# RWKV readout of the state: one f32 product, or three float32r products of split parts

## The chip, the cores and the metric

One core of a Trainium2 chip runs the whole program. The metric is the device time of one execution in microseconds; of the kernel before there are three runs, and one further execution under the hardware profiler. The engines by their names in the profile: PE is TensorE's matmuls, PEld its weight loads, DVE is VectorE, ACT is ScalarE, POOL is GpSimd, SP issues the DMAs.

## What is computed

A linear attention with a decaying state over 768 tokens (4 batches, 8 heads of 48), and behind it two gated feed-forward layers over all 3072 tokens. All inputs are float32.

```python
for t in range(S):
    kt, vt, rt = (k[:, :, t], v[:, :, t], r[:, :, t])
    cur = np.einsum('bhd,bhe->bhde', u[None] * kt, vt)
    y[:, :, t] = np.einsum('bhd,bhde->bhe', rt, state + cur)
    state = w[None, :, :, None] * state + np.einsum('bhd,bhe->bhde', kt, vt)
...
a = x @ w_a
b = x @ w_b
x = a * b @ w_out
...
h = (x @ w1) * (x @ w2) @ w3
return h @ w_out2
```

## The kernel before

The 768 tokens are cut into six steps of 128. A unit `u` (0 to 23) is one batch in one step: step `u // 4`, batch `u % 4`. In a unit each head's work is a masked 128x128 score matrix (`scores`, L380), its product with v (L420), the product of r with the state from the steps before (L416), and the new state (`s_mm`, L481; `s_decay` on ACT, L488; `s_upd` on DVE, L498). Two heads lie side by side in one 112-row tile (rows 0 to 47 and 64 to 111), so the state of a batch is four 112x112 blocks, and L416 is four products of a 112x112 block by 112x128 columns of r. These attention products have plain f32 operands. The products of the feed-forward layers (L631, L684 to L686, L798, L821 to L823) take float32r operands: each float32 tensor is kept as a high part (the value rounded to float32r, written by an ACT cast) and a low part (the rest, written by a DVE subtraction), and a product is the sum of three: high by high, high by low, low by high.

The order of the work is written out by hand. `merge` (L537) goes through the slots of the feed-forward layer's tiles and deals the attention's slots of the next step out between them, so that PE has feed-forward products to do while DVE, ACT and POOL get a unit's operands ready. The eight slots of a unit are in `unit_slots` (L510): scores; masking (`a_evac`, L391) on DVE; writing the diagonal (`a_diag`, L397) on DVE; then, two slots later, `y_mm` and `s_mm` on PE; then the loads of the unit two further on, and `y_evac` on ACT and DVE. Steps 2 to 5 (units 8 to 23) are dealt out over runs with different numbers of slots: in step 2 a unit takes about 10 us, later about 20 us. In these steps POOL prepares the next unit: r by powers of the decay (L352), k likewise (L356), then `k_nat` (L373) and the two products for the diagonal (L361, L363).

`Stream` (L56) brings the feed-forward weights in: a DMA into a staging buffer (`stg_t`, four buffers of 4 KB a partition in the pool `stg`), then an ACT cast and a DVE subtraction (L133, L154). Between its last weight of the first layer, at about 170 us, and its first of the second layer, after 500 us, it does nothing, and the staging buffers are empty. r and k of a unit come in one buffer `rk` (two of them, in turn); the load for unit u+2 (L214, on SP's queue) waits until the last reader of unit u's buffer is done. The tile `at` in PSUM has two buffers and carries scores, y and the state's increment in turn.

Of the kernel before, what the change touches and what calls it, by code (L numbers as in the profile page):

```python
# [8 lines left out]
F32R = mybir.dt.float32r  # L9
# [4 lines left out]
ALU = mybir.AluOpType  # L14
# [4 lines left out]
B, H, S, D = 4, 8, 768, 48  # L19
NP = H // 2  # L20
C = 128
# [7 lines left out]
NF2 = F2 // 128  # L29
NB = NC  # L30
TB = B * C
HALF = C // 2

W_LO, W_HI = 0.72, 1.25
# [142 lines left out]
def rwkv_moe_kernel(ctx, tc, rkT, nat, wu, wab, wout, w12, w3T, wo2, r_in, k_in, v_in, w_in, u_in, out):  # L177
    nc = tc.nc
    mm = nc.tensor.matmul

    dram = ctx.enter_context(tc.tile_pool(name="dram", bufs=1, space=DRAM))
    y_d = dram.tile([B, S, DM], F32, name="y_d")
    m_d = [dram.tile([128, KD, TB], F32, name=f"m_d{q}") for q in range(NB)]

    def flat(ap):
        return ap.rearrange("p a b -> p (a b)")

    with tc.manual_schedule():
# [4 lines left out]
        stg = tc.alloc_tile_pool(name="stg", bufs=Stream.AHEAD, side="right")  # L193
# [16 lines left out]
        def load_rk(u):  # L210
            if u < NU:
                rk_t[u] = (wabp.tile([112, 2, NP * C], F32, tag=("w1h", "w1l", "w2h", "w2l")[u], name="rk")
                           if u < B else att.tile([112, 2, NP * C], F32, name="rk"))
                nc.sync.dma_start(out=rk_t[u], in_=rkT[u])  # L214
# [3 lines left out]
        def load_nat(u):  # L218
            if u < B:
                nc.sync.dma_start(out=v_0[:, u, :], in_=nat[u, :, 2, :])  # L220
            elif u < NU:
                nat_t[u] = att.tile([128, 3, DM], F32, name="natt")
                nc.sync.dma_start(out=nat_t[u], in_=nat[u])
# [101 lines left out]
        nc.vector.tensor_scalar(out=wc, in0=wt, scalar1=W_LO, scalar2=W_HI, op0=ALU.max, op1=ALU.min)  # L325
        zer = const.tile([112, HALF], F32, name="zer")
        nc.vector.memset(zer, 0.0)
        tmp = wabp.tile([112, 1024], F32, tag="w3l", name="tmp")
        pos = tmp[:, 512:512 + NP * (HALF + 1)].rearrange("p (n c) -> p n c", n=NP)
        tkw = tmp[:, 0:512].rearrange("p (n c) -> p n c", n=NP)  # L330
        nc.vector.memset(pos[:, :, 0:1], 1.0)
        for p in range(NP):
            nc.vector.tensor_tensor_scan(
                out=pos[:, p, 1:], data0=wc[:, p:p + 1].to_broadcast([112, HALF]), data1=zer,
                initial=1.0, op0=ALU.mult, op1=ALU.add)
        tr = att.tile([112, NP, C], F32, name="tr", bufs=1)
        nc.vector.tensor_copy(out=tr[:, :, HALF:], in_=pos[:, :, 0:HALF])
        nc.vector.reciprocal(out=tr[:, :, 0:HALF], in_=pos[:, :, 1:][:, :, ::-1])
        tk = att.tile([112, NP, C], F32, name="tk", bufs=1)
        nc.vector.tensor_copy(out=tk, in_=tr[:, :, ::-1])  # L340
        wC = const.tile([112, NP, 1], F32, name="wC")
        nc.vector.tensor_tensor(out=wC, in0=pos[:, :, HALF:], in1=pos[:, :, HALF:], op=ALU.mult)
        s_t = [att.tile([112, NP, 112], F32, name=f"s{b}", bufs=1) for b in range(B)]

        rf_t, d_t, a_t, kn_t, at_ps, xt = {}, {}, {}, {}, {}, {}

        kf_t, pr_t, y3_t = {}, {}, {}

        def prep_r(u, eng):
            r = rk_t[u][:, 0, :]  # L350
# [17 lines left out]
        def k_nat(u):  # L368
            if u < NU - B:
                k = k_0[:, u, :] if u < B else nat_t[u][:, 1, :]  # L370
                kn_t[u] = k if u < B else att.tile([128, DM], F32, name="kn", bufs=1)
                eng = nc.vector if u < 2 * B - 1 else nc.gpsimd
                eng.tensor_tensor(out=kn_t[u], in0=k, in1=tnat.rearrange("p a x d -> p (a x d)"), op=ALU.mult)  # L373

        def scores_f(ps, r, k):

            for p in range(NP):
                s = slice(p * C, (p + 1) * C)
                for x, (r0, r1) in enumerate(XR):
                    mm(ps[x][:, p, :], lhsT=k[r0:r1, s], rhs=r[r0:r1, s], start=True, stop=True)  # L380

        def scores(u):
            for x in range(2):
                at_ps[u, x] = ps_at.tile([128, NP, C], F32, name="at")
            scores_f([at_ps[u, x] for x in range(2)], flat(rf_t[u]), kf_t.pop(u))

        def a_evac(u, hf):
            if hf == 0:
                a_t[u] = (wop.tile([128, H, C], F32, tag=("woh1", "wol1")[u % 2], name="a_0")
                          if u < B else att.tile([128, H, C], F32, name="a_sc", bufs=1))  # L390
            nc.vector.tensor_tensor(  # L391
                out=a_t[u][:, 4 * hf:4 * hf + 4, :], in0=at_ps.pop((u, hf)),
                in1=mask.rearrange("p (o n) -> p o n", o=1).to_broadcast([128, 4, C]), op=ALU.mult)

        def a_diag(u, hf):
            d = d_t[u].rearrange("p (q x) -> p x q", x=2)[:, hf, :]
            nc.vector.copy_predicated(  # L397
                out=a_t[u][:, 4 * hf:4 * hf + 4, :],
                mask=ident.bitcast(I32).rearrange("p (o n) -> p o n", o=1).to_broadcast([128, 4, C]),
                data=d.rearrange("p (h o) -> p h o", o=1).to_broadcast([128, 4, C]))  # L400

        def diag_0(u):

            for x in range(2):
# [2 lines left out]
                    mask=ident.bitcast(I32).rearrange("p (o n) -> p o n", o=1).to_broadcast([128, 4, C]),  # L407
                    data=at_ps.pop(("d", u, x)))

        def y_mm(u):  # L410
            c, b = divmod(u, B)
            ps = at_ps["y", u] = ps_at.tile([112, NP, C], F32, name="at")
            v, a = nat_t[u][:, 2, :], a_t.pop(u)

            for p in range(NP):
                mm(ps[:, p, :], lhsT=s_t[b][:, p, :], rhs=rf_t[u][:, p, :], start=(p == 0), stop=False,  # L416
                   skip_group_check=True)
            for h in range(H):
                r0, r1 = XR[h % 2]
                mm(ps[r0:r1, h // 2, :], lhsT=v[:, h * D:(h + 1) * D], rhs=a[:, h % 2 * 4 + h // 2, :],  # L420
                   start=False, stop=True, skip_group_check=True)
            rf_t.pop(u)
# [16 lines left out]
        def y_0_evac(u):  # L439
            if u == 0:  # L440
                xt[0] = xtp.tile([128, 2, KD, TB], F32R, tag=X_TAG[0], name="xt")
            ps = at_ps.pop(("y", u))
# [4 lines left out]
        def y_evac(u):  # L447
            c, b = divmod(u, B)
            if b == 0:
                xt[c] = xtp.tile([128, 2, KD, TB], F32R, tag=X_TAG[c], name="xt")  # L450
                y3_t[c] = att.tile([112, 2, TB], F32R, name="y3", bufs=1)
            xh, xl = xt[c][:, 0], xt[c][:, 1]
# [8 lines left out]
        def y_shuffle(c):  # L461

            for r0 in (0, 64):
                for k in range(KD):
                    nc.sync.dma_start(out=xt[c][r0 + 48:r0 + 64, :, k, :].bitcast(F32),
                                      in_=y3_t[c][r0 + 16 * k:r0 + 16 * k + 16].bitcast(F32))

        def s_mm(u):
            c, b = divmod(u, B)
            v = v_of(u)  # L470
            nat_t.pop(u, None)
            if c == NC - 1:
                return
            ps = (ps_at.tile([112, NP, D], F32, name="at") if c else
                  ps_m.tile([112, NP, D], F32, tag=("m2", "m0")[u % 2], name="s_ps"))
            at_ps["s", u] = ps
            kn = kn_t.pop(u)
            for p in range(NP):
                for x, (r0, r1) in enumerate(XR):
                    hs = slice((2 * p + x) * D, (2 * p + x + 1) * D)  # L480
                    mm(ps[r0:r1, p, :], lhsT=kn[:, hs], rhs=v[:, hs],  # L481
                       start=True, stop=True)
# [27 lines left out]
        def unit_slots(u):  # L510
            n = u + 1
            nxt = n < NU
            pool = nc.vector if n < 2 * B else nc.gpsimd

            def after(f, *a):
                if nxt:
                    f(n, *a)

            return [
                lambda: (scores(u), after(prep_r, pool)),  # L520
                lambda: (a_evac(u, 0), a_evac(u, 1), after(prep_k, pool)),
                lambda: (a_diag(u, 0), a_diag(u, 1), k_nat(u)),
                lambda: after(prep_d, 0),

                lambda: (y_mm(u), s_mm(u)),
                lambda: (load_rk(u + 2), load_nat(u + 2), y_evac(u), (u + 1) % B == 0 and y_shuffle(u // B), s_decay(u),
                         after(prep_d, 1)),
                lambda: s_upd(u),
                lambda: after(prep_d, 2),
            ]  # L530
# [103 lines left out]
        def ab_slots(x, wget, keep):  # L634
# [3 lines left out]
            def run_a():  # L638
                w, ca, _ = wget()
                t["a"] = ps_ab.tile([128, TB], F32, name="ab")  # L640
                ab_mm(t["a"], w, ca, x())

            def run_b():
                w, _, cb = wget()
                t["b"] = ps_ab.tile([128, TB], F32, name="ab")
                ab_mm(t["b"], w, cb, x())
# [483 lines left out]
```

## Time and profile before

| | us |
|---|---|
| median of three runs | 918.27 |
| the three runs | 917.95, 918.27, 923.23 |
| the profiled execution, its own time | 921.02 |
| its span, first to last instruction | 919.2 |
| PE busy in the span | 889.4 (97%) |
| DVE, ACT, POOL busy | 449.9, 325.2, 106.9 |

The span is what the profile covers; 1.8 us of the profiled execution lie around it. Busy PE time is the union of its records, whose ends are modelled, so distances between starts tell more than durations. One f32 product appears as two PE records (and two weight loads), one float32r product as one of each.

### The profile page before, as it was taken

The numbers are of one execution on the slowest core, as the hardware profiler recorded it, in microseconds if no ns is written. First come the engines' busy times: TensorE is split into PE (matmuls) and PEld (weight loads), VectorE is DVE, ScalarE is ACT, GpSimd is POOL, SyncE is SP. The second block draws the span as 40 slices with busy tenths as digits, with TensorE's granted clock in tenths as the row PEclk, the third lists the DMA queues.
The fourth block names the chain that finished last, engine by engine and source line by source line (L and its number), as shares of the span: only waits on it lengthen the run. The fifth ranks groups of instructions, "written<-read, shape, count | busy, mean of one in ns | idle before, by whom it ended". The sixth has DMA issues, their size and how long they took to land.

```text
span 919.2 us, 12479 instructions
## 1 busy us (share of the span) xinstructions
PE 889.4 (97%) x4962; PEld 754.2 (82%) x4962; DVE 449.9 (49%) x762; ACT 325.2 (35%) x737; POOL 106.9 (12%) x104
## 2 busy tenths in 40 slices
PE   8877999999999999999999999999999999999997
PEld 7665788888888888888888888899988888888886
DVE  8998876356343333433332889566222222223212
ACT  3554565332222232222112778564322222222211
POOL 2204200036033213211100000000000000000000
PEclk9798899999999999999999999999999999999999
DMA  8654531024131221122103555352010101000001
GB/s 263 193 160 138 135 118 63 1 79 154 30 101 46 63 68 59 47 63 81 47 1 109 165 156 172 109 176 71 12 58 11 47 24 47 24 35 1 35 0 38
DMA packets 26065, 73.56 MB, mean 80 GB/s; under 512 B 3152, under 2 KB 7376, under 8 KB 26000
## 3 DMA queue, kind: packets, MB, share of 16 engines
q1 hardware_dynamic: 26000, 72.70, 26.1%
q8 instruction: 41, 0.67, 0.3%
q14 instruction: 24, 0.20, 0.1%
HBM read 61.28 MB, written 9.44 MB: 77 GB/s over the span
## 4 chain that ended last, share of the span: by engine, by line
PE 90%; DVE 6%; issue 1%; DMA 1%; ACT 1%; SPq 0%
PE ab L631 52%; PE m L684 5%; PE m L686 5%; PE m L685 5%; PE at L798 4%; PE o L822 3%; PE o L823 3%; PE o L821 3%; PE at L420 2%; PE at L380 2%; PE at L416 2%; DVE cvt L117 1%; DMA rk<-in_rkT_dram 1%; PE at L823 1%; PE at L821 1%
## 5 line engine op out<-in xcount | busy, mean ns | idle before, releaser
L656 DVE TENSOR_TENSOR ab<-g,ab 128x512 f32<-128x512 f32 x120 | 83.5, 696 | 305.2 <-PE ab L631 272.8
L631 PE MATMUL ab<-xt,w12h 128*128 128x512 f32 x576 | 177.4, 389 | 0.0
L650 ACT COPY g<-ab 128x512 f32<-128x512 f32 x120 | 70.4, 587 | 264.0 <-PE ab L631 263.9
L657 ACT CAST gh<-ab 128x512 fp32r<-128x512 f32 x120 | 70.5, 588 | 253.5 <-DVE ab L656 253.5
L631 PEld LDWEIGHTS ab<-xt,w12h 128*128 128x128 f32 x576 | 107.5, 188 | 18.8
L662 DVE TENSOR_TENSOR gl<-ab,gh 128x512 fp32r<-128x512 f32 x120 | 83.0, 691 | 61.5 <-ACT gh L657 60.8
L631 PE MATMUL ab<-xt,w12l 128*128 128x512 f32 x288 | 112.0, 389 | 0.0
L684 PE MATMUL m<-gh,woh 128*128 128x512 f32 x216 | 85.5, 396 | 0.4 <-ACT woh L133 0.4
L686 PE MATMUL m<-gh,wol 128*128 128x512 f32 x216 | 84.3, 390 | 0.8 <-DVE wol L154 0.8
L685 PE MATMUL m<-gl,woh 128*128 128x512 f32 x216 | 84.3, 390 | 0.0
L631 PEld LDWEIGHTS ab<-xt,w12l 128*128 128x128 f32 x288 | 54.1, 188 | 11.3
L352 POOL TENSOR_TENSOR rk<-rk,tr 112x512 f32<-112x512 f32 x16 | 20.7, 1294 | 281.5 <-DMA rk<-in_rkT_dram 140.3
L631 PE MATMUL ab<-xt,wab0h 128*128 128x512 f32 x144 | 48.0, 415 | 3.1 <-DVE xt L445 2.5
L684 PEld LDWEIGHTS m<-gh,woh 128*128 128x128 f32 x216 | 40.5, 188 | 10.2 <-ACT woh L133 0.8
L686 PEld LDWEIGHTS m<-gh,wol 128*128 128x128 f32 x216 | 40.5, 188 | 9.8 <-DVE wol L154 1.2
L685 PEld LDWEIGHTS m<-gl,woh 128*128 128x128 f32 x216 | 40.6, 188 | 8.3
L631 PE MATMUL ab<-xt,wab1h 128*128 128x512 f32 x144 | 46.9, 408 | 0.0
L631 PE MATMUL ab<-xt,wab4h 128*128 128x512 f32 x144 | 45.5, 397 | 0.0
L631 PE MATMUL ab<-xt,wab3h 128*128 128x512 f32 x144 | 45.5, 397 | 0.0
L631 PE MATMUL ab<-xt,wab2h 128*128 128x512 f32 x144 | 45.4, 397 | 0.0
L631 PE MATMUL ab<-xt,wab5h 128*128 128x512 f32 x144 | 45.0, 394 | 0.0
L117 DVE SCALAR_TENSOR_TENSOR cvt<-stg_t,cvt 128x512 int32<-128x512 int32 x61 | 44.6, 731 | 0.3
(275 smaller groups left out, 1582.2 us busy)
## 6 DMA issues: line engine op xcount, KB each, us to landing
natt<-in_nat_dram SPq DMA_DIRECT2D x20, 576.0 KB, 5.0
rk<-in_rkT_dram SPq DMA_DIRECT2D x24, 448.0 KB, 3.8
stg_t<-in_wab_dram SPq DMA_DIRECT2D x18, 512.0 KB, 4.0
stg_t<-in_w3T_dram SPq DMA_DIRECT2D x16, 512.0 KB, 3.9
stg_t<-in_w_dram SPq DMA_DIRECT2D x12, 512.0 KB, 3.7
stg_t<-in_wout_dram SPq DMA_DIRECT2D x9, 512.0 KB, 3.6
m_d<-m_sb SPq DMA_DIRECT2D x18, 256.0 KB, 3.2
stg_t<-m_d SPq DMA_DIRECT2D x18, 256.0 KB, 2.7
```

The source lines that it names most:

```text
L117: nc.vector.scalar_tensor_tensor(out=f, in0=w[:, :, 1], scalar=-0x40000000, in1=f, op0=ALU.bitwise_and, op1=ALU.bitwise_or)
L631: mm(ps, lhsT=w[i][:, k, cs], rhs=x[:, j, k, :], start=(n == 0), stop=(n == 3 * KD - 1))
L650: nc.scalar.copy(out=t["g"], in_=t["a"])
L656: nc.vector.tensor_tensor(out=t["b"], in0=g, in1=t["b"], op=ALU.mult)
L657: nc.scalar.copy(out=gh, in_=t["b"])
L662: nc.vector.tensor_tensor(out=gl, in0=t["b"], in1=gh, op=ALU.subtract)
L684: mm(m_ps[q][k], lhsT=wh[:, j, cs], rhs=gh, start=first, stop=False)
L685: mm(m_ps[q][k], lhsT=wh[:, j, cs], rhs=gl, start=False, stop=False)
L686: mm(m_ps[q][k], lhsT=wl[:, j, cs], rhs=gh, start=False, stop=last)
L798: mm(f_ps[i], lhsT=w3_t[i][a][:, g, :], rhs=wo2_t[g // 4][b][:, g % 4, :], start=(n == 0), stop=(n == 3 * NF2 - 1))
L821: mm(o_ps[q][b], lhsT=ph[:, cs], rhs=wh, start=(f == 0), stop=False)
L823: mm(o_ps[q][b], lhsT=pl[:, cs], rhs=wh, start=False, stop=(f == NF2 - 1))
```

## The change

From unit 8 on (`RS = 2 * B`) r by the state is computed as three float32r products for each of the four blocks. `split_rs` makes the parts in two tiles of the staging pool: in the slot of the scores ACT casts the state and r to their high parts; in the slot of the masking DVE subtracts for the state's low part; in the slot of the diagonal DVE subtracts for r's low part. Units 4 to 7 keep the f32 product.

```diff
--- before.py
+++ after.py
@@ -29,6 +29,7 @@
 NF2 = F2 // 128
 NB = NC
 TB = B * C
+RS = 2 * B
 HALF = C // 2
 
 W_LO, W_HI = 0.72, 1.25
@@ -344,7 +345,7 @@
 
         rf_t, d_t, a_t, kn_t, at_ps, xt = {}, {}, {}, {}, {}, {}
 
-        kf_t, pr_t, y3_t = {}, {}, {}
+        kf_t, pr_t, y3_t, rs_t = {}, {}, {}, {}
 
         def prep_r(u, eng):
             r = rk_t[u][:, 0, :]
@@ -407,14 +408,34 @@
                     mask=ident.bitcast(I32).rearrange("p (o n) -> p o n", o=1).to_broadcast([128, 4, C]),
                     data=at_ps.pop(("d", u, x)))
 
+        def split_rs(u, part):
+
+            s = s_t[u % B]
+            if part == 0:
+                t = stg.tile([112, 2, NP, 112], F32R, tag="stg_t", name="s_hl")
+                r = stg.tile([112, 2, NP, C], F32R, tag="stg_t", name="r_hl")
+                rs_t[u] = t[:, 0], t[:, 1], r[:, 0], r[:, 1]
+                nc.scalar.copy(out=rs_t[u][0], in_=s)
+                nc.scalar.copy(out=rs_t[u][2], in_=rf_t[u])
+            elif part == 1:
+                nc.vector.tensor_tensor(out=rs_t[u][1], in0=s, in1=rs_t[u][0], op=ALU.subtract)
+            else:
+                nc.vector.tensor_tensor(out=rs_t[u][3], in0=rf_t[u], in1=rs_t[u][2], op=ALU.subtract)
+
         def y_mm(u):
             c, b = divmod(u, B)
             ps = at_ps["y", u] = ps_at.tile([112, NP, C], F32, name="at")
             v, a = nat_t[u][:, 2, :], a_t.pop(u)
 
+            if u < RS:
+                terms = [(s_t[b], rf_t[u])]
+            else:
+                sh, sl, rh, rl = rs_t.pop(u)
+                terms = [(sh, rh), (sh, rl), (sl, rh)]
             for p in range(NP):
-                mm(ps[:, p, :], lhsT=s_t[b][:, p, :], rhs=rf_t[u][:, p, :], start=(p == 0), stop=False,
-                   skip_group_check=True)
+                for i, (s, r) in enumerate(terms):
+                    mm(ps[:, p, :], lhsT=s[:, p, :], rhs=r[:, p, :], start=(p == 0 and i == 0), stop=False,
+                       skip_group_check=True)
             for h in range(H):
                 r0, r1 = XR[h % 2]
                 mm(ps[r0:r1, h // 2, :], lhsT=v[:, h * D:(h + 1) * D], rhs=a[:, h % 2 * 4 + h // 2, :],
@@ -516,10 +537,14 @@
                 if nxt:
                     f(n, *a)
 
+            def rs(part):
+                if u >= RS:
+                    split_rs(u, part)
+
             return [
-                lambda: (scores(u), after(prep_r, pool)),
-                lambda: (a_evac(u, 0), a_evac(u, 1), after(prep_k, pool)),
-                lambda: (a_diag(u, 0), a_diag(u, 1), k_nat(u)),
+                lambda: (scores(u), after(prep_r, pool), rs(0)),
+                lambda: (a_evac(u, 0), a_evac(u, 1), after(prep_k, pool), rs(1)),
+                lambda: (a_diag(u, 0), a_diag(u, 1), k_nat(u), rs(2)),
                 lambda: after(prep_d, 0),
 
                 lambda: (y_mm(u), s_mm(u)),
```

In PE's order around unit 8, the first that is changed, this stands before: the feed-forward product m (`m` from `gh`, `gl` and the weights `woh`, `wol`), r by the state, scores by v, the state's increment, and the next feed-forward product.

```order
L686 MATMUL m_1246<-gh,wol_1451 128x512
L416 MATMUL at<-rk,s_168 112x128 x4
L420 MATMUL at<-a_sc,natt 48x128 x8
L481 MATMUL at<-natt,kn 48x48 x8
L631 MATMUL ab<-xt,wab3h 128x512 x2
```

And now, at the same place:

```order
L711 MATMUL m_1246<-gh,wol_1451 128x512
L437 MATMUL at<-r_hl,s_hl 112x128 x12
L441 MATMUL at<-a_sc,natt 48x128 x8
L502 MATMUL at<-natt,kn 48x48 x8
L656 MATMUL ab<-xt,wab3h 128x512 x2
```

Four f32 products have become twelve float32r products; nothing else on PE has moved. In DVE's order of the same unit (`a_sc` are the masked scores, `ab` and `gl` belong to a feed-forward tile, `y` and `xt` are the unit's output) this stands before:

```order
L391 TENSOR_TENSOR a_sc<-at,mask 128x512 x2
L397 COPY_PREDICATED a_sc<-ident,dg 128x512 x2
L656 TENSOR_TENSOR ab<-g,ab 128x512
L662 TENSOR_TENSOR gl<-ab,gh 128x512
L458 TENSOR_TENSOR y_1733<-at,y_1733 112x128
```

And now:

```order
L392 TENSOR_TENSOR a_sc<-at,mask 128x512 x2
L421 TENSOR_TENSOR s_hl<-s_168,s_hl 112x448
L398 COPY_PREDICATED a_sc<-ident,dg 128x512 x2
L423 TENSOR_TENSOR r_hl<-rk,r_hl 112x512
L681 TENSOR_TENSOR ab<-g,ab 128x512
L687 TENSOR_TENSOR gl<-ab,gh 128x512
L479 TENSOR_TENSOR y_1747<-at,y_1747 112x128
```

One subtraction stands between masking and diagonal, the other behind the diagonal, both ahead of the feed-forward tile's work.

## Rows read from the trace of the kernel before

**Rows 1.** Windows: busy us of each engine, granted clock (PEclk), DMA share, GB/s.

```profile
100.00:120.00 20.00, 18.88 (x82) 14.85 (x81) 19.14 (x27) 13.18 (x33) 6.51 (x5) 1.00 0.60 158
200.00:220.00 20.00, 20.00 (x167) 16.51 (x166) 12.48 (x21) 7.22 (x19) 12.75 (x12) 1.00 0.47 146
```

**Rows 2.** Timeline of PE, units 8 to 11: start us, us, line, tiles, records.

```profile
191.34 1.04 PE L416 MATMUL at<-rk,s 112*112 112x128 f32 x8
...
201.38 1.04 PE L416 MATMUL at<-rk,s 112*112 112x128 f32 x8
...
211.21 0.39 PE L686 MATMUL m<-gh,wol 128*128 128x512 f32 x1
211.44 1.04 PE L416 MATMUL at<-rk,s 112*112 112x128 f32 x8
212.40 1.08 PE L420 MATMUL at<-a_sc,natt 128*48 128x128 f32 x16
...
221.38 1.04 PE L416 MATMUL at<-rk,s 112*112 112x128 f32 x8
222.35 1.34 PE L420 MATMUL at<-a_sc,natt 128*48 128x128 f32 x15
```

**Rows 3.** Line L416: count, and ns of one record (min/median/max).

```profile
L416 PE MATMUL at<-rk,s x160: 270/272/421, 46.2 to 486.9; 112*112 112x128 f32 x160
```

**Rows 4.** Timeline of PE, f32 records with 128 weight and 112 moving columns.

```profile
26.07 0.94 PE L607 MATMUL tn_ps<-ident,tmp 112*128 112x112 f32 x7
```

**Rows 5.** Timeline of PE, float32r records with 384 moving columns.

```profile
584.23 0.85 PE L798 MATMUL at<-wo20l,w30h 128*128 128x384 f32 x4
584.92 0.85 PE L798 MATMUL at<-wo21l,w30h 128*128 128x384 f32 x4
```

**Rows 6.** PEld by line and form: weight loads, busy us, mean ns.

```profile
L631 PEld LDWEIGHTS ab<-xt,w12h 128*128 128x128 f32 x576 | 107.5, 188 | 18.8
```

**Rows 7.** Timeline of DVE, the diagonal's two writes and what follows, units 8 to 11.

```profile
188.41 1.38 DVE L397 COPY_PREDICATED a_sc<-ident,dg 128x512 f32<-128x512 int32 x2
189.67 0.70 DVE L656 TENSOR_TENSOR ab<-g,ab 128x512 f32<-128x512 f32 x1
...
198.36 2.29 DVE L397 COPY_PREDICATED a_sc<-ident,dg 128x512 f32<-128x512 int32 x2
200.55 0.69 DVE L656 TENSOR_TENSOR ab<-g,ab 128x512 f32<-128x512 f32 x1
...
208.40 3.32 DVE L397 COPY_PREDICATED a_sc<-ident,dg 128x512 f32<-128x512 int32 x2
211.61 0.70 DVE L656 TENSOR_TENSOR ab<-g,ab 128x512 f32<-128x512 f32 x1
...
220.51 2.16 DVE L397 COPY_PREDICATED a_sc<-ident,dg 128x512 f32<-128x512 int32 x2
222.56 0.70 DVE L656 TENSOR_TENSOR ab<-g,ab 128x512 f32<-128x512 f32 x1
```

**Rows 8.** Timeline of POOL, units 9 and 10.

```profile
198.55 1.50 POOL L373 TENSOR_TENSOR kn<-natt,tnat 128x384 f32<-128x384 f32 x1
200.01 1.49 POOL L361 TENSOR_TENSOR pr<-natt,u_bc 128x384 f32<-128x384 f32 x1
...
210.10 1.01 POOL L361 TENSOR_TENSOR pr<-natt,u_bc 128x384 f32<-128x384 f32 x1
```

**Rows 9.** Lines L154 and L133: a subtraction and a cast of 512 columns.

```profile
L154 DVE TENSOR_TENSOR w12l<-cvt,w12h x12: 680/689/693, 511.9 to 541.8; 128x512 fp32r<-128x512 f32 x12
...
L133 ACT CAST w12h<-cvt x12: 606/612/642, 509.9 to 541.2; 128x512 fp32r<-128x512 f32 x12
```

**Rows 10.** Waits of SP's queue: who waited for whom, us, times, longest.

```profile
SPq L214 <- PE at L416: 251.1, 14, 46.6
```

**Rows 11.** Timeline of DVE, a unit of step 3.

```profile
244.19 1.37 DVE L397 COPY_PREDICATED a_sc<-ident,dg 128x512 f32<-128x512 int32 x2
```

**Rows 12.** Timeline of PE, the same unit.

```profile
248.15 1.04 PE L416 MATMUL at<-rk,s 112*112 112x128 f32 x8
```

## The prediction

> **What bounds the kernel now.** I read the windows first: in steps 2 to 5 the matmul engine is never idle, and in the stretch in which the first changed units lie it is busy for all 20 of 20.00 us at a granted clock of 1.00, which is the 2.4 GHz level, while DVE is busy for 12.5 us and POOL for 12.8 us [rows 1]. So a microsecond added to PE's row in these steps is a microsecond of the kernel, and work on ACT or DVE costs nothing as long as it is done before PE wants it. Next, PE's timeline for one block of r by the state: eight records, started 110 ns apart (the run is 1.04 us long and its last record 0.27 us: 0.77 us over seven distances), and from the first of them to the first record of scores by v it is 0.96 us (211.44 to 212.40) [rows 2, 3]. Last, the timelines of DVE and POOL just ahead of these blocks, for what the new operands have to fit into [rows 7, 8].
>
> **What is removed and added on PE.** In 16 units (8 to 23) eight f32 records go and twelve float32r records come, each with its weight load of 112 columns. The trace has no float32r product with 128 moving columns; I bound one from four sides.
>
> By the moving side: float32r records with 384 columns start 172 ns apart (0.69 us for four), with 512 columns 230 ns apart (211.21 to 211.44) [rows 2, 5]. A straight line through the two gives 172 - 256 x 58/128 = 56 ns for 128 columns.
>
> By the weights: seven f32 records with 128 weight columns and only 112 moving columns start 112 ns apart (0.94 us less one record of 0.27 us, over six) [rows 4]. By their stream alone they would need 110 x 112/128 = 96 ns, so there the weight load sets the pace, not the stream. If that goes with the weight columns, 112 of them take 112 x 112/128 = 98 ns. The type doesn't change a load: a float32r load of 128 columns is the 188 ns record of the feed-forward products [rows 6].
>
> Like the f32 record that it replaces: 110 ns. If a load can't run beside the record before it: 188 ns, the length of a load's record. Like a float32r record of 512 columns, should short ones be no quicker: 230 ns.
>
> I take 98 ns, because the row that it comes from is the only one that shows a record whose weights outlast its stream, which these are by far. Then the block is eleven distances of 98 ns = 1.08 us and the last record to the next product. That end is 0.96 - 7 x 0.110 = 0.19 us now, and shorter by 110 - 56 = 54 ns with one pass in place of two: 0.14 us. Together 1.22 us instead of 0.96 us, +0.26 us, and for 16 units **+4.2 us**. By the other bounds: 56 ns gives 0.76 us and -3.3 us; 110 ns gives 1.35 us and +6.2 us; 188 ns 2.26 us and +20.8 us (with the whole end of 0.19 us); 230 ns 2.72 us and +28 us.
>
> The page "TensorE: Matmul & The Clock Gate" of the Trainium skill, under LDWEIGHTS, says that a load takes its columns divided by 1.2 in ns, whatever the rows. That is 93 ns for 112 columns and speaks against this change as the rows do; by it the block would be about 55 ns shorter than by mine and the term some 0.9 us smaller.
>
> **What is added on ACT and DVE.** Two casts and two subtractions a unit, of 448 and 512 columns; 512 columns cost ACT 612 ns and DVE 689 ns [rows 9]. ACT casts early, in the slot of the scores, with r ready a unit before; I cost it at nothing, and were this cover gone a late cast would delay the first subtraction by up to 1.2 us. DVE is another matter: the last subtraction must be done before the second product of the block, and it stands behind the masking and the diagonal, in order. What waits for it is PE itself, with everything behind it.
>
> From the start of the diagonal's first write to the block's start there are in units 8 to 11: 191.34 - 188.41 = 2.93 us, 201.38 - 198.36 = 3.02, 211.44 - 208.40 = 3.04, and 221.38 - 220.51 = 0.87 [rows 2, 7]. The two writes alone take 1.26 us (188.41 to 189.67) [rows 7], and the two subtractions add about 1.3 us, so 2.56 us are wanted: by themselves they fit in three of the four units and are 1.69 us late in unit 11.
>
> But POOL works at the same time in units 9 to 11. There the two writes took 2.19, 3.21 and 2.05 us instead of 1.26 (198.36 to 200.55, 208.40 to 211.61, 220.51 to 222.56), and POOL's instructions 1.49 us instead of 1.01 [rows 7, 8]: an instruction of one waits for one of the other. The subtractions read both operands from SBUF too, and I expect the same of them. Unit 9: 0.93 us of such waiting for two instructions, twice that for four: 2.56 + 1.86 - 3.02 = 1.4 us late. Unit 10: here the two writes already waited 1.95 us, and little is left of POOL's work behind them, so that alone: 2.56 + 1.95 - 3.04 = 1.5 us. Unit 11: 2.56 + 0.79 - 0.87 = 2.5 us, of which PE waits about 0.3 us already (its records of scores by v there take 1.34 us instead of 1.08) [rows 2]: 2.2 us. **Waits: 5.1 us.** Between 1.4 us (POOL never in the way: unit 11 alone, 1.69 less 0.3) and 8.4 us (in each of the units 9 to 11 about 1 us more than I took). In steps 3 to 5 there is room: 248.15 - 244.19 = 3.96 us in a unit where the two writes took 1.37 us without POOL beside them [rows 11, 12], so nothing is charged.
>
> The page "SBUF — State Buffer" of the Trainium skill, under "SBUF: two separate sides", says that a DVE instruction with two SBUF inputs and a GpSimd instruction shut each other out for their whole length. The stretched rows agree with that, and by it each of the four instructions could stand behind one whole POOL instruction, which is how the 8.4 us come about.
>
> **DMA and staging.** The load of r and k for unit u+2 waits for the last reader of unit u's buffer; that was the block on PE [rows 10] and is now the subtraction ahead of it, so the load goes a little earlier or as late as PE's new wait; POOL's work moves with it, which is why unit 9's overlap can't be read off exactly. The staging buffers hold no weights in these steps, and the first weights of the second layer come after the last block, so the stream loses nothing.
>
> **Sum.** +4.2 us and +5.1 us = +9.3 us. On the profiled execution's 921.02 us (span 919.2 and 1.8 around it) this is 930.3 us; its time lies 2.75 us over the median of 918.27 us, and on that the forecast is 927.6 us, +1.0%. About 1% (9.2 us) is what a measurement of this kernel can tell from no change.
>
> **The rivals.** *Three passes instead of four* (chance 0.12): the records are bound by the stream, 56 ns apart, the term is -3.3 us, and with waits from 1.4 to 5.1 us the end is between 916.4 and 920.1 us: no slower. For it: one float32r record has half the stream of one f32 record. Against it: the records whose weights outlast their stream [rows 4]. It decides from about 75 ns a record on downward, where a block is no longer than now. The page "FP8 and Floating Point Precision", section TensorE Precision Notes, of the Trainium skill counts a true f32 product as four passes; three for four is what this rival amounts to.
>
> *Waits hidden* (0.18): PE pays 4.2 us, but POOL's work, started earlier, is through before DVE's, and only unit 11 waits: 918.27 + 4.2 + 1.4 = 923.9 us. For it: the earlier load. Against: the load of the operands of L361 comes after the unit's last product, and that is not earlier.
>
> *Short float32r records are dear* (0.13): 188 to 230 ns each, +20.8 to +28 us, with the waits 944 to 951 us. For it: no row shows one shorter than 172 ns. Against: f32 records with loads as long start 110 to 112 ns apart, so loads do overlap.
>
> **How the numbers follow.** The forecast has the remaining 0.57; its own range is 923 to 933 us (waits 1.4 to 8.4, records 98 to 110 ns), about six tenths of it over 1%. Slower by over 1%: 0.34 + 0.13 = 0.47. Faster by over 1%: none of the cases gives it, 0.02 for what I don't see. Within 1%: 0.51. The range from 919.0 to 938.0 us holds the forecast's and the hidden waits' case whole and a third of the first rival; it leaves out the dear records and what lies under it, some 0.2.
>
> **What would show it.** In the changed profile the block's twelve records 98 ns apart and some 1.22 us to the next product in steps 3 to 5; weight loads of about 180 ns that start before the record ahead has ended; PE idle before the block or within its first records in units 9 to 11, ended by a DVE subtraction, and nowhere else; stretched subtractions there. Records 56 ns or 188 ns apart, or PE idle in steps 3 to 5, would make the prediction wrong.

## The result, and the profile after

The changed kernel takes 927.48 us (median of six runs, 925.29 to 928.85) against 918.93 us for the kernel before (six runs, 917.95 to 923.23); the ratio is 1.0069 with a 95% interval of 1.0042 to 1.0095. It is slower, by four to nine microseconds. The medians lie 8.6 us apart and the ratio makes it 6.3 us; single runs of the kernel before scatter over 5 us, so the size of the loss is read from the traces below. The forecast was 927.6 us.

The profiled execution has a span of 927.1 us. PE's timeline shows the changed block; the first rows are units 8 to 11, which answer to [rows 2], the last two unit 12 in step 3, which answer to [rows 12] (columns: start us, us, line, tiles, records, and in brackets the idle time before a row and what ended it).

```profile
191.18 1.30 PE L437 MATMUL at<-r_hl,s_hl 112*112 112x128 f32 x12
...
201.50 0.22 PE L437 MATMUL at<-r_hl,s_hl 112*112 112x128 f32 x1
202.38 1.30 PE L437 MATMUL at<-r_hl,s_hl 112*112 112x128 f32 x11 [0.66 <-DVE r_hl L423]
203.61 0.32 PE L441 MATMUL at<-a_sc,natt 128*48 128x128 f32 x2
...
212.70 0.22 PE L437 MATMUL at<-r_hl,s_hl 112*112 112x128 f32 x1
213.46 1.30 PE L437 MATMUL at<-r_hl,s_hl 112*112 112x128 f32 x11 [0.54 <-DVE r_hl L423]
...
223.66 0.22 PE L437 MATMUL at<-r_hl,s_hl 112*112 112x128 f32 x1
225.29 1.30 PE L437 MATMUL at<-r_hl,s_hl 112*112 112x128 f32 x11 [1.41 <-DVE r_hl L423]
226.52 1.88 PE L441 MATMUL at<-a_sc,natt 128*48 128x128 f32 x16
228.18 0.86 PE L502 MATMUL at<-natt,kn 128*48 128x48 f32 x16
...
253.50 1.30 PE L437 MATMUL at<-r_hl,s_hl 112*112 112x128 f32 x12
254.73 0.32 PE L441 MATMUL at<-a_sc,natt 128*48 128x128 f32 x2
```

Where nothing is waited for (units 8 and 12) a block of twelve records takes 1.23 us from its first record to the first of scores by v; it took 0.96 us [rows 2]. In units 9, 10 and 11 the first product, high by high, runs alone, and the second stands until DVE's subtraction for r's low part (L423) has ended. In the trace these three blocks are 0.88, 0.76 and 1.62 us longer than 1.235 us.

PEld's timeline shows the weight loads of the block in unit 12.

```profile
253.04 0.19 PEld L656 LDWEIGHTS ab<-xt,wab0l 128*128 128x128 f32 x1
253.27 1.39 PEld L437 LDWEIGHTS at<-r_hl,s_hl 112*112 112x112 f32 x12
```

Twelve loads in one unbroken row of 1.39 us; line L437 gives a median of 178 ns for one, so eleven distances of (1.39 less 0.18) / 11 = 110 ns on average. They aren't equal: the first load starts 0.225 us ahead of the second, while the last feed-forward record still runs, and the ten distances behind it are 98 ns each. The records of the products start 96 to 101 ns apart from the third on.

One more stretch has changed. The windows answer to [rows 1] (columns as there: length, PE, PEld, DVE, ACT and POOL busy, granted clock, DMA share, GB/s).

```profile
200.00:220.00 20.00, 18.79 (x156) 15.59 (x155) 13.92 (x23) 9.18 (x23) 11.74 (x9) 1.00 0.43 146
220.00:240.00 20.00, 18.59 (x118) 15.40 (x117) 8.36 (x15) 4.12 (x11) 8.10 (x8) 0.91 0.27 73
240.00:260.00 20.00, 20.00 (x132) 16.59 (x131) 10.71 (x18) 5.68 (x13) 3.51 (x3) 1.00 0.20 66
...
226.80:229.80 3.00, 3.00 (x34) 2.81 (x31) 1.07 (x3) 1.36 (x5) 0.89 (x1) 0.50 0.34 122
```

PE is idle for 1.2 and 1.4 us in step 2, and for about 3 us behind the wait of unit 11 the granted clock is 0.50, the 1.2 GHz level: scores by v take 1.88 us there instead of 1.08 [rows 2], and the state's increment 0.86 us instead of 0.53. From 240 us on PE is full again at 1.00.

DVE's timeline in units 9 and 11, which answers to [rows 7], shows the chain that PE waits for:

```profile
198.45 1.20 DVE L421 TENSOR_TENSOR s_hl<-s,s_hl 112x448 fp32r<-112x448 f32 x1
199.57 1.37 DVE L398 COPY_PREDICATED a_sc<-ident,dg 128x512 f32<-128x512 int32 x2
200.84 1.48 DVE L423 TENSOR_TENSOR r_hl<-rk,r_hl 112x512 fp32r<-112x512 f32 x1
202.25 0.68 DVE L681 TENSOR_TENSOR ab<-g,ab 128x512 f32<-128x512 f32 x1
...
222.79 0.61 DVE L421 TENSOR_TENSOR s_hl<-s,s_hl 112x448 fp32r<-112x448 f32 x1
223.33 1.34 DVE L398 COPY_PREDICATED a_sc<-ident,dg 128x512 f32<-128x512 int32 x2
224.55 0.69 DVE L423 TENSOR_TENSOR r_hl<-rk,r_hl 112x512 fp32r<-112x512 f32 x1
```

and POOL's timeline beside units 9 and 11, which answers to [rows 8]:

```profile
198.15 1.02 POOL L362 TENSOR_TENSOR pr<-natt,u_bc 128x384 f32<-128x384 f32 x1 [0.44 <-DMA natt<-in_nat_dram]
199.25 2.52 POOL L364 TENSOR_TENSOR pr<-pr,natt 128x384 f32<-128x384 f32 x1
...
217.05 1.30 POOL L353 TENSOR_TENSOR rk<-rk,tr 112x512 f32<-112x512 f32 x1 [4.19 <-DMA rk<-in_rkT_dram]
...
221.62 1.02 POOL L364 TENSOR_TENSOR pr<-pr,natt 128x384 f32<-128x384 f32 x1
```

The last two rows are POOL's first and last instruction beside unit 11. It ends at 222.64 us, DVE's first subtraction starts at 222.79, and the subtractions take 0.61 and 0.69 us. In unit 9 they take 1.20 and 1.48 us: the first stands behind L362, the last behind L364, and L364 itself, 1.0 us of work, stands behind the two writes of the diagonal for 1.5 us.

### The profile page after: what moved, and what is told of

Read it like the earlier page. It is cut to its first block, busy times and chain, and to the rows that moved or that the text cites. A ratio compares the mean times of both kernels' runs of the same rounds, so it can differ in the third digit from the quotient of the medians.

```text
span 927.1 us, 12702 instructions
## 1 busy us (share of the span) xinstructions
PE 893.5 (96%) x5026; PEld 759.7 (82%) x5026; DVE 466.5 (50%) x794; ACT 340.6 (37%) x769; POOL 108.3 (12%) x104
## 4 chain that ended last, share of the span: by engine, by line
PE 89%; DVE 7%; DMA 1%; issue 1%; SPq 1%; ACT 1%
PE ab L656 51%; PE m L709 5%; PE m L711 5%; PE m L710 5%; PE at L823 4%; PE o L847 3%; PE o L846 3%; PE o L848 3%; PE at L441 2%; PE at L437 2%; PE at L381 2%; DMA rk<-in_rkT_dram 1%; PE at L848 1%; PE at L846 1%; PE at L847 1%
```

## Accounting in the trace

From the start of unit 8's block to the start of unit 23's, with fifteen blocks between, PE takes 294.83 us in the kernel before and 303.04 us in the changed one: 8.21 us more. Fifteen blocks give 15 x 0.268 = 4.0 us. The other two terms lie in unit 11, between the first record of scores by v and the third row of the feed-forward product behind it. These are the two rows in the changed kernel, in the kernel before and in the run e4 below:

```profile
226.52 1.88 PE L441 MATMUL at<-a_sc,natt 128*48 128x128 f32 x16
230.26 0.62 PE L656 MATMUL ab<-xt,wab5h 128*128 128x512 f32 x2
...
222.35 1.34 PE L420 MATMUL at<-a_sc,natt 128*48 128x128 f32 x15
224.89 0.62 PE L631 MATMUL ab<-xt,wab5h 128*128 128x512 f32 x2
...
223.51 1.08 PE L441 MATMUL at<-a_sc,natt 128*48 128x128 f32 x16
225.68 0.62 PE L656 MATMUL ab<-xt,wab5h 128*128 128x512 f32 x2
```

In e4, at clock 1.00 and with nothing waited for here, the distance is 2.17 us. In the changed kernel it is 3.74 us: the stretch at half clock costs 1.6 us. In the kernel before it is 2.54 us: there scores by v waited for DVE, which cost 0.37 us and is gone now. So the waits give 0.88 + 0.76 + 1.62 = 3.26 us, less 0.37: 2.9 us.

Together that is 8.5 us, 0.25 us more than was measured. These 0.25 us lie behind the blocks of units 12 to 22: from the end of a block to the start of the next one the changed kernel takes 0.01 to 0.02 us less than the kernel before, and 0.09 us less behind unit 20. The same 0.25 us are found in e1, e2, e4, e5 and e7, and not in e6, which keeps the f32 product; so they come with the float32r blocks. Why, the runs don't show.

All runs below are read by the distance from unit 8 to unit 23 too, because their profiles differ ahead of unit 8, in the first 100 us: the block of unit 8 starts anywhere from 187.8 to 191.3 us.

| | unit 8 to unit 23, us | against before |
|---|---|---|
| before | 294.83 | |
| changed | 303.04 | +8.21 |
| e1 parts made a unit earlier | 298.22 | +3.39 |
| e2 from step 3 on | 297.54 | +2.71 |
| e3 half the columns a record | 319.56 | +24.73 |
| e4 two products | 294.99 | +0.16 |
| e5 most of POOL's work out in units 9 to 11 | 299.83 | +5.00 |
| e6 parts made, f32 product | 295.90 | +1.07 |
| e7 two products, parts early | 292.33 | -2.50 |

## The experiments

My theory has two parts: on PE the pace of the weight loads, which each of the sixteen blocks pays, and in step 2 waits for DVE, which are a matter of where the subtractions stand and of POOL. The rivals are that float32r records are slow or quick in themselves, and that the splitting costs wherever it is done. The kernel before was run again beside them, with a median of 920.20 us for e1 to e4 and 920.73 us for e5 to e7; the ratios are to these runs, while the expected times were reckoned from 918.9 and 927.5 us.

**e3: what sets a record's pace.** Each product is cut into two of 64 columns.

```diff
-mm(ps[:, p, :], lhsT=s[:, p, :], rhs=r[:, p, :], ...)
+for c0 in range(0, C, 64):
+    mm(ps[:, p, c0:c0 + 64], lhsT=s[:, p, :], rhs=r[:, p, c0:c0 + 64], ...)
```

> Each float32r product of r by the state is cut into two of 64 moving columns: 24 records and 24 weight loads where there were 12, with the same columns streamed in all. Weight loads set the pace: records stay 98 ns apart, a block takes 23 x 0.098 + 0.11 = 2.4 us instead of 1.235, +18 us over the changed kernel, about 945 us. Rival (the stream or a fixed cost of a few ns per float32r record sets the pace): 50 to 60 ns apart, block about 1.3 us, about 928 us.

Measured 946.1 us (one run, span 944.3). PE's timeline in unit 12:

```profile
256.80 2.46 PE L438 MATMUL at<-r_hl,s_hl 112*112 112x64 f32 x24
259.19 0.32 PE L445 MATMUL at<-a_sc,natt 128*48 128x128 f32 x2
```

2.39 us for 24 records where twelve took 1.23. The same columns are streamed; what has doubled is the records, each with its load, and the block with them. A record with 64 columns costs what one with 128 costs, so the stream isn't the bound at either length. From here the rival of three short passes is out, and so is that of records dear in themselves: they cost 98 ns, not 188 or more.

By itself e3 can't tell the load from a fixed 98 ns for each record, since it doubles both. Two groups of f32 records speak for the load. With 128 weight columns they start 112 ns apart [rows 4], and 98 is to 112 as 112 weight columns are to 128. And the state's increment, with 48 weight columns and 48 moving columns, has sixteen records in 0.53 us (here in unit 12 of the changed kernel; they come in pairs, a pair every 45 ns), so a record as such doesn't cost 98 ns:

```profile
255.64 0.53 PE L502 MATMUL at<-natt,kn 128*48 128x48 f32 x16
```

No run has short float32r records with fewer weight columns; for that type the load as the cause is argued from these rows and not shown.

**e4: fewer records.** The product of the state's low part by r's high part is left out, the part itself is still made.

```diff
-terms = [(sh, rh), (sh, rl), (sl, rh)]
+terms = [(sh, rh), (sh, rl)]
```

> The product of the state's low part by r's high part is left out (the part itself is still made); 8 float32r records a block, as many as the f32 records of the kernel before. Theory: 7 x 0.098 + 0.155 = 0.84 us a block, 0.39 us less than the changed kernel's and 0.13 us less than the f32 block's; the waits of step 2 stay as they are, so 927.5 - 6.3 = 921 us. Rival (float32r records cost a whole f32 record or more each): block 0.96 us or more, 923 us or more.

Measured 921.47 us, ratio 1.0017 (1.0000 to 1.0035). PE's timeline in unit 12, and two windows behind unit 11:

```profile
248.94 0.91 PE L437 MATMUL at<-r_hl,s_hl 112*112 112x128 f32 x8
249.78 0.32 PE L441 MATMUL at<-a_sc,natt 128*48 128x128 f32 x2
```

```profile
220.00:225.00 5.00, 3.44 (x46) 2.92 (x45) 3.92 (x7) 0.94 (x3) 0.33 (x1) 1.00 0.26 70
225.00:230.00 5.00, 5.00 (x22) 4.11 (x23) 2.63 (x6) 1.99 (x6) 3.53 (x3) 1.00 0.72 196
```

0.84 us a block, as expected: eight float32r records are quicker than eight f32 records (0.96 us), and twelve are slower. The waits of units 10 and 11 stayed (0.88 and 1.78 us), and the clock stayed at 1.00 although PE was idle for 1.6 us of the first window. The wait of unit 9 went, which I had not expected: there POOL's L362 started at 197.69 us, 0.47 us behind DVE's subtraction, and this time it was POOL that stood (2.89 us instead of 1.02), while the two subtractions took 0.61 and 0.67 us.

**e1: the parts a unit earlier.** Unit 8 keeps its own slots; the parts of unit u+1 are made in unit u, behind its diagonal and in the two slots after.

```diff
-lambda: (scores(u), after(prep_r, pool), rs(0)),
-lambda: (a_evac(u, 0), a_evac(u, 1), after(prep_k, pool), rs(1)),
-lambda: (a_diag(u, 0), a_diag(u, 1), k_nat(u), rs(2)),
-lambda: after(prep_d, 0),
-lambda: (y_mm(u), s_mm(u)),
+lambda: (scores(u), after(prep_r, pool), own(0)),
+lambda: (a_evac(u, 0), a_evac(u, 1), after(prep_k, pool), own(1)),
+lambda: (a_diag(u, 0), a_diag(u, 1), k_nat(u), own(2), early(0)),
+lambda: (after(prep_d, 0), early(1)),
+lambda: (y_mm(u), s_mm(u), early(2)),
```

> The parts of units 9 to 23 are made in the slots of the unit before (casts behind its diagonal, subtractions in the two slots after it), so that they are done some 5 us or more ahead of the product; the records on PE are those of the changed kernel. Theory (twelve records at the pace of their weight loads, plus waits in step 2 that are only a matter of placing): PE no longer waits for r's low part in units 9 to 11, the clock stays at 1.00 around 227 us, the blocks still take 1.235 us, and 16 x 0.27 = 4.3 us over the kernel before remain: about 923 us. Rival (the splitting work itself costs, wherever it stands, through DVE and POOL): still 926 to 928 us, with waits at other places.

Measured 924.44 us, ratio 1.0043 (1.0026 to 1.0060). PE's timeline in unit 10, and the windows:

```profile
210.17 1.30 PE L437 MATMUL at<-r_hl,s_hl 112*112 112x128 f32 x12
211.40 0.43 PE L441 MATMUL at<-a_sc,natt 128*48 128x128 f32 x4
```

```profile
200.00:220.00 20.00, 20.00 (x174) 16.74 (x173) 16.31 (x24) 9.20 (x23) 11.40 (x10) 1.00 0.42 129
220.00:240.00 20.00, 20.00 (x132) 16.59 (x131) 10.58 (x17) 5.29 (x12) 6.38 (x5) 1.00 0.28 69
```

No wait, no stretch at the lower clock, and the blocks as long as before: what is left, +3.39 us from unit 8 to 23, is the records (4.0 us) less the 0.37 us that the kernel before waited in unit 11 and the 0.25 us behind the later blocks: 3.4 us. DVE does the same subtractions, one of them stretched to 2.75 us, and nothing waits for them.

**e2: from step 3 on.** Units 8 to 11 keep the f32 product.

```diff
-RS = 2 * B
+RS = 3 * B
```

> The change applied from unit 12 on only; units 8 to 11 keep the f32 product. Theory: no wait is left, since all of them are in step 2, and 12 x 0.27 = 3.2 us remain: about 922 us. Rival (the splits cost time in every step): 12/16 of the whole loss, about 925 us.

Measured 923.31 us, ratio 1.0034 (1.0016 to 1.0051); +2.71 us in the trace, with eleven changed blocks between the two marks (11 x 0.268 = 2.95, less the 0.25 us behind them). PE waits for no subtraction, so the waits are step 2's alone.

**e5: POOL's part in the waits.** Three of POOL's five instructions are left out in units 9 to 11.

```diff
 def prep_d(u, part):
+    if u in LEFT and part < 2:
+        pr_t[u] = nat_t[u][:, 0, :].rearrange("p (h d) -> p h d", h=H)
...
 def k_nat(u):
+    if u + 1 in LEFT:
+        kn_t[u] = nat_t[u][:, 1, :]
```

> The changed kernel with three of POOL's five instructions left out in units 9 to 11 (the state's k is not scaled there, and the diagonal of units 10 to 12 is summed from r alone). POOL is then through before DVE's subtractions start. Theory (in units 9 and 10 the waits come from POOL and DVE standing in each other's way, in unit 11 from DVE's own chain): the subtractions take 0.61 and 0.69 us there instead of 1.1 to 1.5, PE's waits of 0.88 and 0.76 us in units 9 and 10 are gone, that of 1.6 us in unit 11 stays. From 100 us to the end the kernel then loses 8.5 - 1.6 = 6.9 us on the kernel before, or 5.5 if the stretch at the half clock does not come. Rival (DVE's additional work alone makes all three waits): they stay.

Measured 922.82 us (one run). DVE's timeline in unit 10, and the waits for r's low part in units 8 to 11 (us in all, times, longest):

```profile
205.41 0.62 DVE L427 TENSOR_TENSOR s_hl<-s,s_hl 112x448 fp32r<-112x448 f32 x1
205.95 1.36 DVE L404 COPY_PREDICATED a_sc<-ident,dg 128x512 f32<-128x512 int32 x2
207.21 0.67 DVE L429 TENSOR_TENSOR r_hl<-rk,r_hl 112x512 fp32r<-112x512 f32 x1
```

```profile
PEld at L443 <- DVE r_hl L429: 1.7, 1, 1.7
PE at L443 <- DVE r_hl L429: 1.4, 1, 1.4
```

One wait is left of three, that of unit 11, as long as it was. So the waits of units 9 and 10 are POOL's and DVE's standing in each other's way, and that of unit 11 is DVE's own chain, too long for the 0.87 us that the order of the slots leaves it. The clock stayed at 1.00 here too.

**e6: the splitting alone.** All parts are made, and the product stays f32.

```diff
-terms = [(sh, rh), (sh, rl), (sl, rh)]
+terms = [(s_t[b], rf_t[u])]
```

> The parts are made as in the changed kernel, but the product stays the f32 product of the unsplit operands. Theory (casts and subtractions cost only where PE waits for them): block 0.967 us, no wait for r's low part, at most some tenths of a us for the diagonal in units 9 to 11: no difference from the kernel before beyond 0.1%. Rival (the additional work on ACT, DVE and SBUF costs by itself): 3 us or more over it.

Measured 919.43 us, ratio 0.9990 (0.9972 to 1.0009). In the time no difference, but in the trace +1.07 us, and I had allowed some tenths. PE's timeline shows where, at the scores of unit 10:

```profile
204.45 0.46 PE L381 MATMUL at<-rk 48*128 48x128 f32 x2
205.54 1.13 PE L381 MATMUL at<-rk 48*128 48x128 f32 x14 [0.62 <-DVE s L519]
```

The scores need a tile `at` that DVE frees with the update of the state (L519). In this run the state's subtraction of unit 9 took 2.44 us beside POOL, and DVE was late with all that followed. Where PE doesn't meet the lateness at the product, it meets it at the next scores, as far as it is still there.

**e7: a version that is quicker than both.** e1 with the state's low part left out altogether: the state enters the product rounded to float32r, r keeps both parts.

```diff
-terms = [(sh, rh), (sh, rl), (sl, rh)]
+terms = [(sh, rh), (sh, rl)]
```

> The parts made early as in e1, and the state's low part left out altogether (the state enters rounded to float32r): 8 float32r records a block. Theory: no waits, block 0.842 us instead of 0.967, 16 x 0.125 = 2.0 us and a wait of 0.25 us in unit 11 less than the kernel before: 0.998 of its time. Rival (float32r records don't gain on f32 ones in place): 1.000 or more.

Measured 916.14 us, ratio 0.9959 (0.9939 to 0.9978), -2.50 us in the trace: fifteen blocks of 0.842 us instead of 0.967 make 1.88 us, the wait of unit 11 that is gone 0.37 us, and the 0.25 us behind the later blocks come here too. PE's timeline in unit 12:

```profile
245.27 0.91 PE L437 MATMUL at<-r_hl,s_hl 112*112 112x128 f32 x8
246.12 0.54 PE L441 MATMUL at<-a_sc,natt 128*48 128x128 f32 x6
```

It computes less than either kernel, so it stands beside them only where the rounding of the state is allowed.

## Why the prediction was right, and where its parts were off

**The bound.** PE is busy without a gap wherever the new operands are in time (units 8 and 12 on), and each block's 0.27 us is found again at the end. Right.

**The records.** 98 ns from the row in which weights outlast the stream; the trace has 96 to 101 ns, the block 1.235 us instead of 1.22, the term 16 x 0.268 = 4.3 us instead of 4.2. That the block came so near is in part luck: the second record starts only 0.06 us behind the first, and the last one starts 0.19 us ahead of scores by v, where I had taken 98 ns and 0.14 us. That the pace is the loads' rests on e3 and [rows 4] together. The page "TensorE: Matmul & The Clock Gate" of the Trainium skill (LDWEIGHTS: columns divided by 1.2) gives an estimate of 93 ns for 112 columns, some 5 ns short of what was measured. The 56 ns of the straight line through the longer float32r records were no use below the length at which the loads take over.

**The waits.** The places were right (units 9 to 11, ended by the subtraction for r's low part, none in steps 3 to 5), the sizes too large: 0.9, 0.8 and 1.25 us (1.62 less 0.37) instead of 1.4, 1.5 and 2.2, together 2.9 instead of 5.1. (For the wait that the kernel before already had in unit 11 I had taken 0.3 us.) The step that failed is the waiting that I charged for all four of DVE's instructions in unit 9, and for units 10 and 11 as it was: in the trace only the two subtractions waited, once each, the diagonal's writes ran at their full pace while POOL stood, and by unit 11 POOL had finished. Its work there begins when the load of r and k has landed, and that load now waits for the subtraction ahead of unit 10's block and no longer for the block on PE (SP's queue waited for L423 14 times, 209.8 us in all, where it had waited for L416 [rows 10]). POOL's first row beside unit 11 in the kernel before is:

```profile
216.05 1.29 POOL L352 TENSOR_TENSOR rk<-rk,tr 112x512 f32<-112x512 f32 x1 [3.50 <-DMA rk<-in_rkT_dram]
```

So POOL begins 223.66 - 217.05 = 6.6 us ahead of unit 11's block, and not 221.38 - 216.05 = 5.3 us ahead of it as before. I had named this shift and not worked it into the waits. The page "SBUF — State Buffer" of the Trainium skill (SBUF: two separate sides) says that a DVE instruction with two SBUF inputs and a GpSimd instruction that reads SBUF shut each other out for a whole instruction. The stretched rows agree with that (1.20 and 1.48 us instead of 0.61 and 0.69 on DVE, 2.52 instead of 1.02 on POOL). The upper bound of 8.4 us that rested on one whole POOL instruction for each of DVE's was far too high: in unit 9 two of the four stood, and POOL stood behind the other two.

**What was missing.** The stretch at the 1.2 GHz level behind unit 11, 1.6 us. I had counted PE's waits at their own length. So the sum is nearer than its parts, and that is luck: 4.2 + 5.1 = 9.3 us was forecast, and 4.3 + 2.9 + 1.6, less 0.25, = 8.5 us came; the waits were forecast 2.2 us too large, and that made up for the 1.6 us that the forecast didn't have. The forecast ratio of 1.010 lies just outside the interval's upper end of 1.0095, the time of 927.6 us within the runs.

**ACT.** The casts were put at nothing, and nothing in the trace waits for them. Right.

**The rivals.** Three passes instead of four: out by e3. Dear short records: out by the 98 ns. Hidden waits: POOL was through ahead of DVE in unit 11 alone. Two of the three waits could be hidden (e5) and all three can (e1), but where the change put the subtractions they weren't.

## What to carry to other kernels

Where a product has few moving columns, count the records with their weight loads, not passes: here a record cost 98 ns with 64 columns and with 128, and three float32r products of one record each, in the place of one f32 product of two, put twelve loads where eight were. Before an operand is made one slot ahead of its use, measure the room from the start of the last thing ahead of it on that engine to the use, unit by unit (2.9, 3.0, 3.0 and 0.87 us here), and look at what runs beside it: here POOL stretched a subtraction of 0.61 us to 1.20. A unit earlier the same work cost PE nothing, though one subtraction took 2.75 us there. And a wait on PE can cost more than its length, as that of 1.4 us did here, with 1.6 us behind it.

## What the runs showed that I had not expected

The granted clock fell to 0.50 for about 3 us behind a wait of 1.4 us on PE in the changed kernel, and in e3 there is such a stretch behind the same wait (0.68 on average from 230 to 235 us). It did not fall in e4 (wait of 1.6 us) or e5 (1.4 us). What separates them these runs don't settle; no run was made for it.

In nine profiles of kernels whose order is the same up to there, the block of unit 8 starts between 187.8 and 191.3 us. This scatter comes from the first 100 us and is over four tenths of the effect that was to be measured. From unit 8 on, a block with nothing to wait for takes the same time in every run of the same form, to a few hundredths of a microsecond.
